# The shift inside the softmax exponentials of an attention kernel: an immediate 4 in place of a column per head

## The chip, the cores and the metric

The kernel runs on one core of a Trainium2 chip, as one launch. The metric is the device time of that launch in microseconds. The engines of the core are named as in the profile: PE (TensorE, matrix multiplications), PEld (its weight loads), ACT (ScalarE, activations), DVE (VectorE), POOL (GpSimd) and SP (SyncE, which here only issues DMAs). SBUF is the working memory, 128 partitions wide; PSUM, in 8 banks of 128x512 fp32, is what PE writes to.

## The reference

Two blocks read the same x (2048 tokens of 1024 numbers) and a gate mixes them:

```python
g = _sigmoid((x * gate_w).sum(-1, keepdims=True))
a = _A_ref(x, A_wqkv, A_wo)          # attention, 32 heads of 32 numbers
b = _B_ref(x, B_w_q, B_k1, B_k2, B_u, B_v)   # a router over 64 experts
return g * a + (1 - g) * b
```

The part that matters here is the attention:

```python
scores = jnp.einsum("bhqd,bhkd->bhqk", q, k) * (Dh ** -0.5)
p = _softmax(scores, axis=-1)
o = jnp.einsum("bhqk,bhkd->bhqd", p, v)
```

A softmax does not change when the same number is taken from all scores of a row. The kernel takes no maximum of the scores: it computes exp(score - shift) with a shift known ahead, adds the rows up, and divides by the sum at the end.

## The kernel before

All is fp32. The stages run one after the other: projections to q and k, router, projections to v (up to some 645 us of the span), attention (to some 1840 us), output projection (to the end). The scheduling is by hand: the order of the Python calls is the order of each engine's queue.

**The shift and the branch.** While q and k are evacuated, `evac` keeps the greatest absolute value of each of their rows in `amax`. The products of the two, spread by head over columns (`prf`), are summed over a head's 32 rows by a product with ones in `bound` (L450 to L455): the sum bounds every score of the head, before the scale. `bound` writes this bound, times minus the scale, into a column per head of `shift`, on all 128 partitions: four matmuls fill the four groups of 32 partitions, and an ACT copy scales them. It also writes the greatest bound of all heads to `cbits`. At the end of the program (L1456) `cbits` is loaded into a register and compared, as bits, with a limit: if a bound is above 30 after the scale, `exact` computes the attention again with true maxima. With the reference's inputs the greatest bound is 2.77, or 0.49 after the scale (worked out from the inputs).

**The attention loop** (L1083) makes 16 steps for each of the 32 heads. A step calls `unit(h, i)`, a chunk of 512 queries times four blocks of 128 keys:

- `score` issues 12 PE matmuls (L819), four at a time in different row groups of the array, into four banks of a ring of seven PSUM banks (`ring`).
- `weigh` issues the ACT exponentials (L825) from the ring into the SBUF tiles `P`. A unit has 2048 columns: two exponentials of 512 and one of 1024, or four of 512 where the ring wraps inside the last pair. This is the instruction whose bias operand is `shift[:, h:h + 1]`.
- `pv` multiplies one earlier P tile by V (L940), two steps late. At step 2 of a head it is left out, and `head_sums` puts the row sums of the head before the last one into a ring bank instead (L950), from where DVE copies them (L987, `ssb`); step 3 then makes two `pv`.

There are eight P buffers, used in turn, and each step takes one more, so a P tile must be free again about 6.5 steps after it is full. Until then `pv` has read it, and its row sums have been taken along. `presum` does that in one of two ways: DVE adds the tile to an accumulator (`acc`, L964 and L966), or, for three tiles of each head, POOL issues a DMA that adds it to a second accumulator in SBUF (`accd`, L959). In most heads tile 1 is the second accumulator itself, and tiles 6, 11 and 15 are added to it, each such DMA after the one before has landed. `merge` (L969) adds the two accumulators, 6 steps into the next head.

**The queue of SP** carries, in this order within a head: the store of the finished head's output (`od`, after the ACT copy `osb`, L980), the store of row sums (`smd`, after the DVE copy `ssb`), eight loads of K and Q for the next head (256 KB each, onto 32 partitions each), and a load of V; in heads 8 to 23 two 128-partition loads of `wo` too. Once in four heads, `load_r` reads the row sums of the four heads back (`rr`), and at step 8 `norm_r` on DVE takes their reciprocals (L998 to L1000) and SP stores them (`rd`). A head with `norm_r` in the queue of DVE, together with the head after it, is called a turn below: heads 5 and 6, 9 and 10, and so on, seven times in the loop.

Of the kernel before, what the change touches and what calls it, by code (L numbers as in the profile page):

```python
# [9 lines left out]
F32 = mybir.dt.float32  # L10
F32R = mybir.dt.float32r
I32 = mybir.dt.int32
AF = mybir.ActivationFunctionType
# [5 lines left out]
H = 32  # L19
# [5 lines left out]
W = 256  # L25
SCALE = 32 ** -0.5

SHIFT_LIMIT = 30.0


@with_exitstack
def gated_mha_peer_kernel(ctx, tc, xT, wqkv, wv, wo, wq, k12, ug, v, out):
# [8 lines left out]
    nc = tc.nc  # L41
# [3 lines left out]
    const = ctx.enter_context(tc.tile_pool(name="const", bufs=1))  # L45
# [19 lines left out]
    ones = const.tile([128, 32], F32, name="ones")  # L65
    nc.vector.memset(ones, 1.0)
    G64 = const.tile([128, 64], F32, name="G64")
    cbits = const.tile([1, 1], F32, name="cbits")
    shift = const.tile([128, H], F32, name="shift")


    const.tile([128, 56], F32, name="fill")
# [32 lines left out]
    def bank():  # L105
        i = bank_no[0] % 8
        bank_no[0] += 1
        return ps1.tile([128, 512], F32, name=f"bk{i}")
# [215 lines left out]
    for k, (w, c) in enumerate(chunks):  # L324
        hi, lo = whl.pop((w, c))
        for n in range(NQ):
            ps = bank()
# [44 lines left out]
    prf = prm.rearrange("p c j -> p (c j)")  # L372
# [76 lines left out]

    def bound():  # L450
        pb = bank()
        for i in range(4):
            nc.tensor.matmul(pb[32 * i:32 * i + 32, :H], ones, prf, start=True, stop=True)
        nc.vector.tensor_reduce(cbits, pb[:1, :H], axis=AX.X, op=OP.max)
        nc.scalar.activation(shift, pb[:, :H], AF.Copy, scale=-SCALE)  # L455

    def gate_sums():
        pz = bank()
# [26 lines left out]
    for t in range(NT - 1):  # L485
        router_mm(t)
        router_step(t)
        if t == 4:
            bound()
            load_wv(0, "xh0")  # L490
            load_wv(1, "xl0")
        if t == 5:
            gate_sums()
            rz.close()
        if t >= 8 and t % 2 == 0:
            ni, ki = divmod(t // 2 - 4, 2)
            in_parts(f"B{ki + 1}{2 - ni}", x_place(f"x{'hl'[ki]}{1 + ni}"), WR[ki, 1 - ni])
# [244 lines left out]
    def values_unit(u):  # L742
# [10 lines left out]
        for k, name in enumerate(order):  # L753
# [6 lines left out]
            if last and name == "P2":  # L760
                first_scores()
# [42 lines left out]
    P, pools = {}, {}  # L804

    def p_tile(h, kt):

        i = pools["next"] % 8
        pools["next"] += 1
        P[h, kt] = pools["left" if i >= 4 else "right"].tile([128, S], F32, name=f"P{i}")  # L810
        return P[h, kt]

    def score(K, Q, p, c, banks, on=lambda ins, *_: ins):

        for i in range(3):
            for r in range(4):
                k0, q0 = 1024 * (i == 2) + 128 * p, 1024 * (i == 1) + 512 * c
                rows = slice(32 * r, 32 * r + 32)
                on(nc.tensor.matmul(banks[r], K[rows, k0:k0 + 128], Q[rows, q0:q0 + 512],  # L819
                                    start=(i == 0), stop=(i == 2)), r)  # L820

    def weigh(h, tiles, c, r, m, src):

        dst = tiles[r // 2].rearrange("p (b s) -> p b s", b=2)[:, r % 2:r % 2 + m, 512 * c:512 * c + 512]
        return nc.scalar.activation(dst, src, AF.Exp, bias=shift[:, h:h + 1], scale=SCALE)  # L825

    def first_scores():

        tp.close()
        pools.update(right=Pool("ppr", side="right"), next=0)  # L830
        tiles = [p_tile(0, i) for i in range(2)]
        banks = [ps1.tile([128, 512], F32, name=f"bk{i}") for i in (5, 6, 0, 1)]
        score(*Z, 0, 0, banks)
        for r, ps in enumerate(banks):
            weigh(0, tiles, 0, r, 1, ps[:, None, :])

    def pv_bank():
        return pso.tile([128, 512], F32, name="o")
# [41 lines left out]
    ring = pss.tile([128, NB, 512], F32, name="ring")  # L880
# [3 lines left out]
    def ring_banks(n):  # L884
        i = [(ring_no[0] + k) % NB for k in range(n)]
        ring_no[0] += n
        return i

    def on_ring(ins, *banks):

        for other, theirs in users:
            if ins.ins.engine != other.ins.engine and not theirs & set(banks):
                tc.declare_no_dep(ins.ins, other.ins, reason="different banks of the ring")
        users.append((ins, set(banks)))
        del users[:-18 * NB]
# [19 lines left out]
    def unit(h, i):  # L915


        m, c = divmod(i, 2)
        banks = ring_banks(4)
        score(*KQ[h % 2], m, c, [ring[:, k, :] for k in banks], lambda ins, r: on_ring(ins, banks[r]))  # L920
        for p in (2 * m, 2 * m + 1):
            if c == 0 and p == sums_of(h)[0]:
                P[h, p] = ACCD[h] = wk.tile([128, S], F32, name="accd")
            elif c == 0:
                p_tile(h, p)
        cuts = sorted({1, 2, 4} | {r for r in range(1, 4) if banks[r] == 0})
        r0 = 0
        for r1 in cuts:
            k = banks[r0]
            on_ring(weigh(h, [P[h, 2 * m], P[h, 2 * m + 1]], c, r0, r1 - r0, ring[:, k:k + r1 - r0, :]),  # L930
                    *range(k, k + r1 - r0))
            r0 = r1

# [10 lines left out]
    def sums_of(h):  # L944
        return (2, 4, 6) if h == H - 1 else (2, 6, 11, 15) if h == 0 else (1, 6, 11, 15)
# [117 lines left out]
    for k in range(2 * KC):  # L1063
        c = slice(k % 2 * D // 2, (k % 2 + 1) * D // 2)
# [18 lines left out]
    for s in range(H * NT):  # L1083
        h, i = divmod(s, NT)
        if s > 0:
            unit(h, i)
        if h >= 2 and i == LAG - 1:
            head_sums(h - 2)
        elif s + 1 >= LAG:
            for _ in range(1 + (h >= 2 and i == LAG)):  # L1090
                next_pv()
        if h == H - 1 and i == 8:
            head_sums(h - 1)
        for f, a in todo.pop(s, []):
            f(*a)
        if i % 2:
            for p in (i - 1, i):
                presum(h, p)
# [240 lines left out]
    for n in range(2, S // W):  # L1339
        unit(n)  # L1340
# [112 lines left out]
        gps.close()  # L1453
        gate.close()

    limit_bits = int(np.float32(SHIFT_LIMIT / SCALE).view(np.int32))  # L1456
    creg = nc.values_load(cbits.bitcast(I32), min_val=0, max_val=2 ** 31 - 1,
                          skip_runtime_bounds_check_because="a float's bits without its sign")
    with tc.If(creg > limit_bits):
# [29 lines left out]
```

## Time and profile before

| | |
|---|---|
| median of 3 runs | 2027.85 us (2026.49 to 2029.06) |
| the profiled execution | 2027.6 us, of which the span (first to last instruction) is 2025.8 us |
| granted TensorE clock, mean | 0.995 |
| PE busy | 1974.6 us, 97% |
| ACT busy | 1338.1 us, 66% |
| DVE busy | 1384.6 us, 68% |
| POOL busy | 171.1 us, 8% |
| exponentials into P from the ring (L825) | x1530, 1074.4 us |
| exponentials into accd from the ring (L825) | x77, 84.5 us |

How to read the lines quoted below: a group line gives the source line, the engine, the operation, what is written and read, the shapes, the count, then busy time in us, the mean duration of one in ns, and the idle time of the engine just before them with what ended it. A timeline line gives the start in us of the span, the time to the end of the merged instructions, the engine, the line and the count; in brackets stands idle time before it and what ended it. Durations of consecutive ACT instructions overlap, so the rate of ACT is read from their starts. A window line gives, for a stretch of the span, its length, the busy time of each engine (with its count of instructions), the granted clock, the mean busy share of the 16 DMA engines (it may pass 1, since a packet's time includes some waiting) and GB/s.

### The profile page before, as it was taken

Reading aid. Unit: us, or ns where it says so; the run is one execution under the profiler, and the core shown is the slowest. Engines: PE = TensorE matmul, PEld = TensorE weight load, DVE = VectorE, ACT = ScalarE, POOL = GpSimd, SP = SyncE. Lnnn points to the kernel's source line nnn. Section 1 sums busy time; section 2 is a strip of 40 time slices with the busy share of each in tenths; the row PEclk is TensorE's granted clock in tenths of the full one; section 3 lists DMA queues with packets and bytes.
Section 4 is the critical chain, followed back from the end, with each engine's and each line's share of the span. In section 5 each row is a group of like instructions: output and inputs, shape, how many; then the busy total and the mean of one; then the engine's idle time right before and its main releaser. Section 6 shows DMA issues by size and latency. Waiting matters only on the chain. (4 is left out here: it accounts for less than half of the span.)

```text
span 2025.8 us, 34915 instructions
## 1 busy us (share of the span) xinstructions
PE 1974.6 (97%) x14227; PEld 1079.8 (53%) x14227; DVE 1384.6 (68%) x1254; ACT 1338.1 (66%) x1973; POOL 171.1 (8%) x218
## 2 busy tenths in 40 slices
PE   9999999999999999999999999999999999999998
PEld 7877778878886333333333333333333333336786
DVE  4522227779867777687688688678688688677574
ACT  4211112112333999999999999989999999995221
POOL 0000000055011000000000000000000000001000
PEclk9999999999999999999999999999999999999999
DMA  5777754221377878878778789778788787875961
GB/s 197 272 277 278 270 210 143 93 84 58 127 237 242 168 143 170 154 152 169 152 164 174 154 166 172 152 167 170 149 175 159 156 169 159 158 161 164 277 184 54
DMA packets 125361, 348.47 MB, mean 172 GB/s; under 512 B 16852, under 2 KB 57188, under 8 KB 99464
## 3 DMA queue, kind: packets, MB, share of 16 engines
q1 hardware_dynamic: 86680, 195.40, 36.3%
q0 software_dynamic: 17904, 112.99, 27.5%
q10 hardware_dynamic: 20608, 37.76, 5.2%
q8 instruction: 114, 1.87, 0.4%
q14 instruction: 55, 0.45, 0.1%
HBM read 174.90 MB, written 71.57 MB: 122 GB/s over the span
## 5 line engine op out<-in xcount | busy, mean ns | idle before, releaser
L825 ACT ACTIVATE P<-ring,shift 128x512 f32<-128x512 f32 (+1 forms) x1530 | 1074.4, 914 | 50.8 <-issue 23.1
L966 DVE TENSOR_TENSOR acc<-acc,P 128x2048 f32<-128x2048 f32 x319 | 731.0, 2292 | 74.9 <-ACT P L825 51.6
L940 PE MATMUL o<-P,V 128*32 128x512 f32 x3840 | 515.2, 608 | 2.5 <-DMA V<-vd 1.4
L819 PE MATMUL ring<-z,z 32*128 32x512 f32 x3060 | 324.8, 441 | 23.6 <-DVE ssb L987 15.9
L819 PE MATMUL ring<-Q,K 32*128 32x512 f32 x3072 | 322.5, 438 | 10.4 <-ACT P L825 8.5
L819 PEld LDWEIGHTS ring<-z,z 32*128 32x128 f32 x3060 | 169.8, 185 | 282.3 <-ACT P L825 119.2
L819 PEld LDWEIGHTS ring<-Q,K 32*128 32x128 f32 x3072 | 169.1, 183 | 266.9 <-ACT P L825 123.2
L95 ACT ACTIVATE hi<-bk 128x512 fp32r<-128x512 f32 x64 | 37.6, 599 | 242.9 <-PE bk L331 231.2
L331 PE MATMUL bk<-xh,whi 128*128 128x512 f32 x448 | 176.3, 394 | 0.1
L331 PE MATMUL bk<-xh,wlo 128*128 128x512 f32 x448 | 174.6, 390 | 0.0
L331 PE MATMUL bk<-xl,whi 128*128 128x512 f32 x448 | 174.6, 390 | 0.0
L959 POOL DMA_DIRECT2D accd<-P x95 | 81.5, 858 | 1089.7 <-ACT P L825 817.3
L940 PEld LDWEIGHTS o<-P,V 128*32 128x32 f32 x3840 | 76.2, 108 | 180.8 <-issue 164.9
L96 DVE TENSOR_TENSOR lo<-bk,hi 128x512 fp32r<-128x512 f32 x64 | 44.1, 690 | 182.2 <-ACT hi L95 178.5
L964 DVE TENSOR_TENSOR acc<-P,P 128x2048 f32<-128x2048 f32 x32 | 73.3, 2291 | 70.3 <-ACT P L825 64.5
L331 PEld LDWEIGHTS bk<-xh,whi 128*128 128x128 f32 x448 | 84.1, 188 | 24.1 <-issue 6.7
L331 PEld LDWEIGHTS bk<-xh,wlo 128*128 128x128 f32 x448 | 84.1, 188 | 17.6
L331 PEld LDWEIGHTS bk<-xl,whi 128*128 128x128 f32 x448 | 84.2, 188 | 16.8
L825 ACT ACTIVATE accd<-ring,shift 128x1024 f32<-128x1024 f32 (+1 forms) x77 | 84.5, 1142 | 0.0
L969 DVE TENSOR_TENSOR acc<-acc,accd 128x2048 f32<-128x2048 f32 x32 | 73.2, 2286 | 1.8 <-DMA accd<-P 1.8
L987 DVE COPY ssb<-ring 128x512 f32<-128x512 f32 x31 | 21.4, 690 | 72.6 <-ACT osb L980 62.6
L564 PE MATMUL pa<-woh,acc 128*128 128x512 f32 x192 | 62.6, 391 | 1.1 <-ACT acc L95 0.8
(242 smaller groups left out, 1858.7 us busy)
## 6 DMA issues: line engine op xcount, KB each, us to landing
accd<-P POOLq DMA_DIRECT2D x95, 1024.0 KB, 8.3
wqt<-in_wq SPq DMA_DIRECT2D x32, 1024.0 KB
z<-kd SPq DMA_DIRECT2D x64, 256.0 KB
z<-qd SPq DMA_DIRECT2D x64, 256.0 KB
K<-kd SPq DMA_DIRECT2D x64, 256.0 KB
Q<-qd SPq DMA_DIRECT2D x64, 256.0 KB
V<-vd SPq DMA_DIRECT2D x32, 256.0 KB
od<-osb SPq DMA_DIRECT2D x32, 256.0 KB
```

Of the source, the lines that this page charges most:

```text
L95: nc.scalar.activation(hi, src, AF.Copy)
L96: (on or nc.vector).tensor_tensor(out=lo, in0=src, in1=hi.bitcast(F32), op=OP.subtract)
L331: nc.tensor.matmul(ps, a[:, kc, :], b[n][:, kc, :], start=first, stop=last)
L564: nc.tensor.matmul(ps, self.a[a][i][:, k, :], self.b[b][j][k], start=(not first and k == 0 and i == j == 0), stop=(k == HC - 1 and i == 1))
L819: on(nc.tensor.matmul(banks[r], K[rows, k0:k0 + 128], Q[rows, q0:q0 + 512], start=(i == 0), stop=(i == 2)), r)
L825: return nc.scalar.activation(dst, src, AF.Exp, bias=shift[:, h:h + 1], scale=SCALE)
L940: nc.tensor.matmul(O[h][32 * qc:32 * qc + 32, :], Vt[g][:, kt, 32 * j:32 * j + 32], P[h, p][:, qc * 512:(qc + 1) * 512], start=(p == 0), s ...
L959: nc.gpsimd.dma_start(ACCD[h], P[h, kt], accum_op=OP.add)
L964: nc.vector.tensor_add(ACC[h], P[h, 0], P[h, kt])
L966: nc.vector.tensor_add(ACC[h], ACC[h], P[h, kt])
L969: nc.vector.tensor_add(ACC[h], ACC[h], ACCD[h])
L987: ins = copy(o, ps)
```

## The change

The exponentials take the immediate -4 as their bias for every head. The tile `shift` (128 bytes per partition) is gone, with the ACT copy that filled it and three of the four matmuls in `bound`; the one left makes only row 0, which `cbits` needs. The limit that the branch at the end tests is 4 after the scale, in place of 30. Since the bound is 0.49, the branch is not taken before or after the change.

```diff
-SHIFT_LIMIT = 30.0
+SHIFT = 4.0
...
-    shift = const.tile([128, H], F32, name="shift")
...
     def bound():
         pb = bank()
-        for i in range(4):
-            nc.tensor.matmul(pb[32 * i:32 * i + 32, :H], ones, prf, start=True, stop=True)
+        nc.tensor.matmul(pb[:1, :H], ones[:, 0:1], prf, start=True, stop=True)
         nc.vector.tensor_reduce(cbits, pb[:1, :H], axis=AX.X, op=OP.max)
-        nc.scalar.activation(shift, pb[:, :H], AF.Copy, scale=-SCALE)
...
-    def weigh(h, tiles, c, r, m, src):
+    def weigh(tiles, c, r, m, src):
...
-        return nc.scalar.activation(dst, src, AF.Exp, bias=shift[:, h:h + 1], scale=SCALE)
+        return nc.scalar.activation(dst, src, AF.Exp, bias=-SHIFT, scale=SCALE)
...
-            weigh(0, tiles, 0, r, 1, ps[:, None, :])
+            weigh(tiles, 0, r, 1, ps[:, None, :])
...
-            on_ring(weigh(h, [P[h, 2 * m], P[h, 2 * m + 1]], c, r0, r1 - r0, ring[:, k:k + r1 - r0, :]),
+            on_ring(weigh([P[h, 2 * m], P[h, 2 * m + 1]], c, r0, r1 - r0, ring[:, k:k + r1 - r0, :]),
...
-    limit_bits = int(np.float32(SHIFT_LIMIT / SCALE).view(np.int32))
+    limit_bits = int(np.float32(SHIFT / SCALE).view(np.int32))
```

## The prediction

> **What bounds the kernel now.** I read the page first, then the groups by shape, then the timelines of ACT, PE and POOL inside the attention loop, then the stretches of one head.
>
> ```profile
> span 2025.8 us, 34915 instructions
> PE 1974.6 (97%) x14227; PEld 1079.8 (53%) x14227; DVE 1384.6 (68%) x1254; ACT 1338.1 (66%) x1973; POOL 171.1 (8%) x218
> ACT  4211112112333999999999999989999999995221
> ```
>
> PE is busy in all stages, but a busy PE may be one that waits inside. ACT is nearly full in 23 of the 40 slices only, and these are the attention loop. The change touches its exponentials, so the loop is the stage to read. The exponentials by shape:
>
> ```profile
> L825 ACT ACTIVATE P<-ring,shift 128x512 f32<-128x512 f32 x1144 | 761.7, 805 | 50.8 <-issue 23.1 <-ACT P L825 14.5 <-DMA accd<-P 7.0
> L825 ACT ACTIVATE P<-ring,shift 128x1024 f32<-128x1024 f32 x386 | 477.6, 1237 | 0.0
> L825 ACT ACTIVATE accd<-ring,shift 128x1024 f32<-128x1024 f32 x51 | 66.2, 1298 | 0.0
> L825 ACT ACTIVATE accd<-ring,shift 128x512 f32<-128x512 f32 x26 | 18.3, 837 | 0.0
> ```
>
> That is 1170 of 512 columns and 437 of 1024. Their mean durations include time behind the one before, so the price of one is read from start to start:
>
> ```profile
> 757.35 1.16 ACT L825 ACTIVATE accd<-ring,shift 128x1024 f32<-128x1024 f32 x1
> 758.35 1.33 ACT L825 ACTIVATE P<-ring,shift 128x512 f32<-128x512 f32 x2
> 759.49 1.34 ACT L825 ACTIVATE accd<-ring,shift 128x512 f32<-128x512 f32 x2
> 760.63 0.69 ACT L980 ACTIVATE osb<-o 128x512 f32<-128x512 f32 x1
> 761.11 1.37 ACT L825 ACTIVATE P<-ring,shift 128x512 f32<-128x512 f32 x2
> ```
>
> An exponential of 1024 takes 1.00 us (757.35 to 758.35), one of 512 takes 0.57 (two in 758.35 to 759.49, two more to 760.63). The Copy `osb`, same shape, also from PSUM to SBUF, but with immediates only, takes 0.48 (760.63 to 761.11). So ACT needs (1170 x 0.57 + 437 x 1.00) / 32 + 0.48 = 35.0 us per head.
>
> PE in a step at the pace of ACT, and then in the steps of another head after ACT has caught up:
>
> ```profile
> 1001.58 1.24 PE L819 MATMUL ring<-Q,K 32*128 32x512 f32 x12
> ...
> 1003.74 1.38 PE L819 MATMUL ring<-Q,K 32*128 32x512 f32 x12
> ```
> ```profile
> 797.55 1.06 PE L950 MATMUL ring<-acc,ones 128*32 128x512 f32 x8
> 798.55 0.50 PE L819 MATMUL ring<-z,z 32*128 32x512 f32 x2
> ...
> 800.78 1.06 PE L940 MATMUL o<-P,V 128*32 128x512 f32 x8
> 801.66 1.04 PE L940 MATMUL o<-accd,V 128*32 128x512 f32 x8
> 802.63 0.97 PE L819 MATMUL ring<-z,z 32*128 32x512 f32 x12
> 803.53 1.06 PE L940 MATMUL o<-P,V 128*32 128x512 f32 x8
> 804.53 0.98 PE L819 MATMUL ring<-z,z 32*128 32x512 f32 x12
> ```
>
> A step at ACT's pace takes 2.16 us (1001.58 to 1003.74); a free step takes 1.90 (802.63 to 804.53), 0.90 for the scores and 1.00 for `pv`. PE's own need per head is 16 x 0.90 + 14 x 1.00 + 1.00 (the sums, 797.55 to 798.55) + 1.85 (the two `pv` of step 3, 800.78 to 802.63) = 31.25 us. Now the actual length of a head, from the accumulating DMAs that POOL issues, and the restart of ACT:
>
> ```profile
> 811.72 0.86 POOL L959 DMA_DIRECT2D accd<-P  x1 [14.70 <-ACT P L825]
> 826.26 0.86 POOL L959 DMA_DIRECT2D accd<-P  x1 [13.69 <-DMA accd<-P]
> 833.73 0.86 POOL L959 DMA_DIRECT2D accd<-P  x1 [6.61 <-ACT P L825]
> 848.43 0.86 POOL L959 DMA_DIRECT2D accd<-P  x1 [13.84 <-ACT P L825]
> ...
> 887.35 0.86 POOL L959 DMA_DIRECT2D accd<-P  x1 [15.83 <-ACT P L825]
> ...
> 923.63 0.86 POOL L959 DMA_DIRECT2D accd<-P  x1 [15.71 <-ACT P L825]
> ```
> ```profile
> 825.84 2.27 ACT L825 ACTIVATE P<-ring,shift 128x512 f32<-128x512 f32 x3 [0.31 <-DMA accd<-P]
> ```
>
> The issues at 811.72, 848.43, 887.35 and 923.63 are those of tile 6 in four heads. Two of the three distances are regular, 36.7 and 36.3 (I take 36.5); the middle one, 38.9, is a turn. A head thus takes 1.5 us over ACT's 35.0: ACT is the bound, with small waits. One of them is a warning. At 825.84, step 14, ACT had waited for the DMA of tile 6, issued at 811.72: its buffer is the one that step 14 writes. That wait is 0.31 us now, so this DMA lands just when the present pace needs it.
>
> **The change part by part.** *The exponentials.* Each loses its operand in SBUF: 0.57 - 0.48 = 0.09 us, if Exp and Copy differ in nothing else. 1607 x 0.09 = 145 us of ACT, 4.5 per head, leaves 30.5. ACT is then below PE's 31.25, so at most 36.5 - 31.25 = 5.2 us of a head can be won. The ends: if the difference belongs to Exp and not to the column, the saving is 0; above 0.075 (3.75 us over 50 exponentials of a head) PE is the bound and more brings nothing. I take 0.09, since shape, source and destination are the same in both rows.
>
> *What is late next: DVE.* Adds per head:
>
> ```profile
> L966 DVE TENSOR_TENSOR acc<-acc,P 128x2048 f32<-128x2048 f32 x319 | 731.0, 2292 | 74.9 <-ACT P L825 51.6 <-DVE acc L966 0.9
> ...
> L964 DVE TENSOR_TENSOR acc<-P,P 128x2048 f32<-128x2048 f32 x32 | 73.3, 2291 | 70.3 <-ACT P L825 64.5 <-PE ring L950 3.1 <-DMA vd<-xh 2.8
> L969 DVE TENSOR_TENSOR acc<-acc,accd 128x2048 f32<-128x2048 f32 x32 | 73.2, 2286 | 1.8 <-DMA accd<-P 1.8
> ```
>
> (731.0 + 73.3 + 73.2) / 32 = 27.4 us, under 31.25: no bound in a regular head.
>
> *What is late next: the DMAs.* One head, from a landing of tile 6 (restart at 825.84) to the next one:
>
> ```profile
> 825.80:835.00 9.20, 9.01 (x84) 3.33 (x80) 5.64 (x3) 9.16 (x14) 1.71 (x2) 1.00 0.56 114
> 835.00:845.00 10.00, 9.66 (x92) 3.41 (x88) 6.58 (x4) 9.31 (x15) 0.00 (x0) 1.00 1.01 213
> 845.00:855.00 10.00, 10.00 (x100) 4.03 (x97) 7.68 (x4) 10.00 (x15) 0.86 (x1) 1.00 1.06 190
> 855.00:862.20 7.20, 7.20 (x69) 2.62 (x68) 0.00 (x0) 7.20 (x11) 0.00 (x0) 1.00 0.55 105
> ```
>
> The share times the length adds up to 5.2 + 10.1 + 10.6 + 4.0 = 29.8 us of full engines per head, close to PE's 31.25. And it cannot be packed evenly: after a landing, the DMAs of tiles 11 and 15 go one after the other (826.26, 833.73), 8 us at a share of 0.56 that no faster ACT shortens. After these 8 us the remaining 29.8 - 4.5 = 25.3 run at 1.03 at best (the two middle rows): 24.5 us, so a head of 32.5. If the thin tail of 7.2 us at 0.55 stays too, it costs 3.2 more: 35.7.
>
> The landing of tile 6 from its issue: now the issue comes 848.43 - 825.84 = 22.6 us after the restart. ACT has nine and a half steps and an `osb` in between, 9.5 x 30.0 / 16 + 0.5 = 18.3 us in the future, PE about 19 (nine steps at 1.90, the sums, the double `pv`). So the issue moves to about 19 us, ahead of some of the loads of K, Q and V that it follows today. With today's 14.1 us to landing (811.72 to 825.84) that gives a head of 33.1. I take 33.7 for a regular head, between this and the middle of the two bounds (34.1): **2.8 us less, in 24 heads, 67 us.**
>
> [...]
>
> *A turn.* DVE stands before the reciprocals, and PE's ring bank waits for DVE:
>
> ```profile
> 862.25 0.20 DVE L998 TENSOR_SCALAR rr<-rr 128x64 f32<-128x64 f32 x1 [9.46 <-DMA rr<-smd]
> ...
> 877.74 0.69 DVE L987 COPY ssb<-ring 128x512 f32<-128x512 f32 x1
> ```
> ```profile
> 878.48 0.96 PE L819 MATMUL ring<-z,z 32*128 32x512 f32 x10 [2.51 <-DVE ssb L987]
> ```
>
> `rr` lands with the accumulation (862.25), and 16.2 us of queued DVE adds pass until PE goes on (878.48); neither gets shorter. Of the other 22.7 us some eight and a half steps shrink by 0.26: **2.2 us, in 7 turns, 15 us.**
>
> *The last head* has its accumulations early (tiles 4 and 6); 18 steps and the drain at 0.26 give **5 us**. *The rest*:
>
> ```profile
> L453 PE MATMUL bk<-prm,ones x8: 196/207/218, 419.5 to 419.6; 128*32 128x32 f32 x8
> ```
>
> Six of these eight passes go, all within 0.3 us, and an ACT Copy of 32 columns; **0.4 us** at most, nothing at least. The tiles behind `shift` lie 128 bytes lower; no row prices that, and I take 0. The branch costs the same, as it isn't taken.
>
> Sum: 2027.6 - 67 - 15 - 5 - 0.4 = 1940 us, against the profiled execution, which lies 0.25 us under the median.
>
> **The rivals.** *PE alone is the bound* (the accumulation, issued early, lands in time): a regular head 31.7 with a little friction, 4.8 us less in 24; a turn 3.5 less; 5 at the end: 2027.6 - 115 - 25 - 5 = 1882. For it: free steps of 1.90 do occur; against: 29.8 us of DMA in 31.7.
>
> *The accumulation's landing is pinned* 36.4 us after the one before, whatever the issue: 0.1 to 0.3 us in 24 heads, 15 in the turns, 5 at the end: 2027.6 - 5 - 20 = 2003. For it: the restart at 825.84 shows ACT on that DMA already, and all 16 engines are full from 835 to 855; against: its issue moves ahead of loads.
>
> *Slower: every head becomes a turn.* The output's store then comes 1.1 us earlier after a landing, beside the DMA of tile 15; if this one lands so late that `merge` blocks DVE for over 6 us, DVE's queue holds the ring bank as at 877.74, and a regular head takes 38.9: 24 x 2.4 = 58 us more, 5 less at the end, 2080. Against: `merge` has waited for it 1.8 us in total.
>
> *The change doesn't do what it says* (the -4 still comes from a column): 2027.
>
> A longer wait also touches the clock:
>
> ```profile
> 1328.00:1332.00 4.00, 4.00 (x28) 1.26 (x28) 2.12 (x2) 2.46 (x4) 0.00 (x0) 0.56 0.98 236
> ```
>
> After a turn's wait the granted clock was 0.56 for 4 us. [...]
>
> **How the numbers follow.** Forecast 0.50 (1915 to 1970: heads of 32.5 to 35), PE alone 0.19, pinned 0.23, no effect 0.03, slower 0.05. The range from 1885 to 2003 reaches both neighbours. About 4 us (0.2%) can be told from no change: faster 0.92, the same 0.03, slower 0.05.
>
> **What would show it.** Exponentials 0.48 us from start to start (0.91 for 1024); ACT's idle time going from `issue` to the DMA of `accd`; tile 6 issued some 19 us after a landing; a regular head of 33.7; steps of 1.90 on PE. I am wrong if the exponentials keep 0.57, if heads are 31.7 with no wait on `accd`, or if tile 6 lands 36 us after the one before.

## The result, and the profile after

The changed kernel takes 1977.1 us (median of 4 runs, 1974.5 to 1980.7), the kernel before 2028.5 us (median of 4): a ratio of 0.975, with a 95% interval of 0.973 to 0.977. 51 us were won; 88 had been forecast, with a range of 1885 to 2003. The profiled execution of after took 1980.73 us with a span of 1978.9 us, 46.9 us less than the profiled execution of before.

The head of the page of after, then the share of the chain of waits by what it ran through:

```profile
span 1978.9 us, 34902 instructions
PE 1894.2 (96%) x14221; PEld 1023.2 (52%) x14221; DVE 1384.7 (70%) x1254; ACT 1201.4 (61%) x1972; POOL 171.2 (9%) x218
ACT  4211112101423898978988888888889888895221
...
DMA accd<-P 11%; PE ring L816 10%; PE o L937 9%; PE pa L561 6%; DVE acc L963 4%; DMA rr<-smd 4%; ACT P L822 3%; DMA z<-kd 2%; PE ring L947 1%; DMA od<-osb 1%; DMA wo_raw<-t1l 1%; DMA accd<-rd 1%; PE pa L1136 1%; DMA smd<-ssb 0%; ACT accd L822 0%
```

ACT is busy 1201 us in place of 1338, 137 us less, and is no longer full in the loop. The chain's largest part is now the DMA that adds to `accd`. The exponentials in the timeline of ACT:

```profile
784.99 1.11 ACT L822 ACTIVATE accd<-ring 128x1024 f32<-128x1024 f32 x1
785.89 1.19 ACT L822 ACTIVATE P<-ring 128x512 f32<-128x512 f32 x2
786.85 1.15 ACT L822 ACTIVATE accd<-ring 128x1024 f32<-128x1024 f32 x1
787.75 0.74 ACT L977 ACTIVATE osb<-o 128x512 f32<-128x512 f32 x1
788.23 4.07 ACT L822 ACTIVATE P<-ring 128x512 f32<-128x512 f32 x6
```

One of 1024 columns takes 0.90 us (784.99 to 785.89, and 786.85 to 787.75), one of 512 takes 0.48 (two in 785.89 to 786.85), as long as the Copy `osb` (787.75 to 788.23). The saving of 0.09 us is there in full. What ACT does with it shows in the groups, where the first idle time is now the DMA's:

```profile
L822 ACT ACTIVATE P<-ring 128x512 f32<-128x512 f32 (+1 forms) x1530 | 939.1, 766 | 144.9 <-DMA accd<-P 61.1
```

Before, 7.0 us of ACT's waits in the loop were for that DMA; now it is 61.1. One head in the timelines of POOL and ACT, from a restart to the next one:

```profile
800.38 0.86 POOL L956 DMA_DIRECT2D accd<-P  x1 [11.14 <-ACT P L822]
815.38 0.86 POOL L956 DMA_DIRECT2D accd<-P  x1 [14.14 <-DMA accd<-P]
822.74 0.86 POOL L956 DMA_DIRECT2D accd<-P  x1 [6.50 <-ACT accd L822]
835.15 0.86 POOL L956 DMA_DIRECT2D accd<-P  x1 [11.56 <-ACT P L822]
```
```profile
814.96 3.90 ACT L822 ACTIVATE P<-ring 128x512 f32<-128x512 f32 x6 [1.62 <-DMA accd<-P]
...
849.56 5.03 ACT L822 ACTIVATE P<-ring 128x512 f32<-128x512 f32 x8 [2.34 <-DMA accd<-P]
```

Tile 6 is issued at 800.38 and 835.15, a head of 34.8 us. From the restart at 814.96 to the issue are 20.2 us (22.6 before), from the issue to the next restart, at 849.56, 14.4. There are 30 such waits of ACT in the loop, and in most heads PE waits with it. By their place in the loop 22 are for tile 6, at step 14, and 8 for tile 15 of the head before, at step 8; the longest of the 30, 4.5 us, is one of these 8.

The stretches from one issue of tile 6 to the next, for seven of the thirty heads; after the length come the busy times of PE, PEld, DVE, ACT and POOL, then the granted clock, the DMA share and GB/s:

```profile
835.15:877.36 42.21, 36.10 (x332) 12.38 (x328) 29.33 (x18) 31.44 (x51) 2.57 (x3) 0.92 0.80 169
877.36:909.57 32.21, 32.21 (x340) 11.17 (x332) 27.35 (x13) 31.20 (x53) 2.57 (x3) 1.00 0.76 162
909.57:944.73 35.16, 32.61 (x332) 11.31 (x328) 28.02 (x14) 31.18 (x52) 2.58 (x4) 1.00 0.78 142
944.73:979.22 34.49, 33.25 (x332) 11.60 (x330) 28.10 (x14) 31.36 (x53) 2.58 (x3) 1.00 0.84 175
...
1051.12:1087.53 36.41, 34.09 (x336) 11.70 (x332) 28.08 (x14) 31.37 (x53) 2.57 (x3) 0.95 0.80 169
...
1195.82:1234.87 39.05, 35.05 (x332) 12.06 (x331) 27.74 (x14) 31.53 (x53) 2.57 (x4) 0.91 0.82 175
...
1411.86:1454.20 42.34, 37.31 (x332) 12.56 (x328) 29.43 (x18) 31.62 (x52) 2.57 (x3) 0.88 0.80 169
```

The lengths go with the clock. Of the 23 regular heads, 16 ran at a full clock and took 33.5 us on average: nine of about 34.5 like 944.73, six that follow a turn and take about 32.3 like 877.36 (in five of them PE is busy from end to end), and the loop's first, of 31.3. Six heads with a clock of 0.95 took 36.4 on average, and one with 0.91 took 39.1. In before, all 23 regular heads had a clock of 1.00 and took 36.3. The seven turns took 40.5 us (40.0 before), at clocks between 0.88 and 0.96.

How a head loses its clock, in PE's timeline of one regular head, and the clock of the stretches around it:

```profile
1063.89 0.50 PE L816 MATMUL ring<-Q,K 32*128 32x512 f32 x3
1066.71 1.09 PE L816 MATMUL ring<-Q,K 32*128 32x512 f32 x9 [2.32 <-ACT P L822]
1067.73 1.94 PE L937 MATMUL o<-P,V 128*32 128x512 f32 x8
1069.59 1.51 PE L816 MATMUL ring<-z,z 32*128 32x512 f32 x12
```
```profile
1064.00:1067.40 3.40, 1.08 (x12) 0.56 (x12) 3.30 (x2) 1.34 (x3) 0.86 (x1) 1.00 0.15 46
1067.40:1070.80 3.40, 3.40 (x25) 1.04 (x20) 2.47 (x2) 2.56 (x4) 0.00 (x0) 0.50 0.93 193
```

PE waits 2.32 us for ACT, which waits for the DMA. From 1067.40 on the clock is 0.50 for 3.4 us: a `pv` that takes 1.00 us elsewhere takes 1.86 (1067.73 to 1069.59). In a turn it is worse:

```profile
861.66 0.50 PE L816 MATMUL ring<-z,z 32*128 32x512 f32 x2
866.39 1.65 PE L816 MATMUL ring<-z,z 32*128 32x512 f32 x10 [4.24 <-DVE ssb L984]
867.97 1.94 PE L937 MATMUL o<-P,V 128*32 128x512 f32 x8
869.83 1.65 PE L816 MATMUL ring<-z,z 32*128 32x512 f32 x12
871.41 1.75 PE L937 MATMUL o<-P,V 128*32 128x512 f32 x8
873.09 0.97 PE L816 MATMUL ring<-z,z 32*128 32x512 f32 x12
```

The wait for `ssb` is 4.24 us where it was 2.51, and the two steps behind it take 3.44 and 3.26 us in place of 1.90: 2.9 us lost. In the record of the clock the loop of after has 17 such stretches, 75 us in all; the loop of before has 3, 14 us in all.

### The profile page after: what moved, and what is told of

Same layout as the page of the kernel before. It is cut to its first block, busy times and chain, and to the rows that moved or that the text cites. A ratio compares the mean times of both kernels' runs of the same rounds, so it can differ in the third digit from the quotient of the medians.

```text
span 1978.9 us, 34902 instructions
## 1 busy us (share of the span) xinstructions
PE 1894.2 (96%) x14221; PEld 1023.2 (52%) x14221; DVE 1384.7 (70%) x1254; ACT 1201.4 (61%) x1972; POOL 171.2 (9%) x218
## 3 DMA queue, kind: packets, MB, share of 16 engines
q1 hardware_dynamic: 86680, 195.40, 36.1%
## 4 chain that ended last, share of the span: by engine, by line
PE 27%; DMA 19%; DVE 5%; ACT 3%; issue 2%; SPq 0%; DVEq 0%; ACTq 0%; POOLq 0%
DMA accd<-P 11%; PE ring L816 10%; PE o L937 9%; PE pa L561 6%; DVE acc L963 4%; DMA rr<-smd 4%; ACT P L822 3%; DMA z<-kd 2%; PE ring L947 1%; DMA od<-osb 1%; DMA wo_raw<-t1l 1%; DMA accd<-rd 1%; PE pa L1136 1%; DMA smd<-ssb 0%; ACT accd L822 0%
## 5 line engine op out<-in xcount | busy, mean ns | idle before, releaser
L822 ACT ACTIVATE P<-ring 128x512 f32<-128x512 f32 (+1 forms) x1530 | 939.1, 766 | 144.9 <-DMA accd<-P 61.1
L937 PE MATMUL o<-P,V 128*32 128x512 f32 x3840 | 528.6, 623 | 2.7 <-DMA V<-vd 1.8
L816 PE MATMUL ring<-z,z 32*128 32x512 f32 x3060 | 281.1, 443 | 35.2 <-DVE ssb L984 19.3
L816 PE MATMUL ring<-Q,K 32*128 32x512 f32 x3072 | 277.1, 434 | 31.3 <-ACT P L822 31.1
L816 PEld LDWEIGHTS ring<-z,z 32*128 32x128 f32 x3060 | 141.8, 191 | 284.2 <-ACT P L822 138.3
L816 PEld LDWEIGHTS ring<-Q,K 32*128 32x128 f32 x3072 | 139.6, 186 | 274.1 <-ACT P L822 153.5
L822 ACT ACTIVATE accd<-ring 128x1024 f32<-128x1024 f32 (+1 forms) x77 | 72.3, 973 | 0.0
L984 DVE COPY ssb<-ring 128x512 f32<-128x512 f32 x31 | 21.4, 689 | 62.0 <-PE ring L947 48.1
```

What stands on the lines that cost most here:

```text
L822: return nc.scalar.activation(dst, src, AF.Exp, bias=-SHIFT, scale=SCALE)
L937: nc.tensor.matmul(O[h][32 * qc:32 * qc + 32, :], Vt[g][:, kt, 32 * j:32 * j + 32], P[h, p][:, qc * 512:(qc + 1) * 512], start=(p == 0), s ...
L984: ins = copy(o, ps)
```

## The experiments

Medians are of four to seven executions each (one in the last two runs), ratios against the kernel before on the same chip (2027.4, 2028.8 and 2029.3 us).

### Is it the immediate, or one of the other edits?

The kernel after, with the -4 in a column of 128 rows that is set once:

```diff
+    shift = const.tile([128, 1], F32, name="shift")
+    nc.vector.memset(shift, -SHIFT)
...
-        return nc.scalar.activation(dst, src, AF.Exp, bias=-SHIFT, scale=SCALE)
+        return nc.scalar.activation(dst, src, AF.Exp, bias=shift, scale=SCALE)
```

> The changed kernel with all its edits but one: the bias of the exponentials comes from a column of -4 in SBUF, filled once by a memset. Theory (the immediate alone makes the difference; the value of the shift, the smaller bound() and the limit nothing): 2024 to 2032 us, as the kernel before. Rival (the value, the addresses or bound() take part): below 2015 us.

2034.3 us, ratio 1.002 (1.000 to 1.004). The whole gain is gone although everything else of the change stayed: the new limit of the branch and the smaller `bound` win nothing.

### Is the accumulating DMA the new bound?

The kernel after (first run) and the kernel before (second run) without the three DMA additions of each head. The row sums of those tiles are left out of the computation.

```diff
         if kt in sums:
-            nc.gpsimd.dma_start(ACCD[h], P[h, kt], accum_op=OP.add)
             return
```

> The changed kernel without the DMAs that add tiles 6, 11 and 15 of each head (4 and 6 of the last) to the second accumulator: their row sums are left out of the output's divisor. Theory (after the change a head waits for the landing of tile 6, since the DMA engines are full): the waits go and a head falls from some 35 us to PE's need of 31.25 and a little, the time to 1860 to 1895 us. Rival (the wait for the landing only stands where PE, the clock or ACT would have made another one): 1955 to 1980 us.

> The kernel before, with the column, without the same DMAs (the same row sums are left out). Theory (ACT is the bound of the kernel before, at 35.0 us a head): 1965 to 2000 us, so that between this one and the one without a column lie 90 us or more, against 51 with the DMAs in place. Rival (DMAs were already the bound before): it falls to within 60 us of the one without a column.

Without them after takes 1863.8 us (0.919, interval 0.917 to 0.920) and before 1996.2 (0.984, 0.983 to 0.986). With no DMA to wait for, the immediate is worth 132 us, close to the 145 us of ACT that it saves; with the DMAs it is worth 51. The additions cost the kernel before 31 us and the kernel after 113.

The mean granted clock of after without them is 0.998 (0.979 with them), and 1.00 over its loop (640 to 1680). Its heads take 32.1 us, not the 31.25 that I had added up for PE. Step 3 in PE's timeline, and PE's weight loads there:

```profile
777.50 1.06 PE L947 MATMUL ring<-acc,ones 128*32 128x512 f32 x8
778.50 1.88 PE L816 MATMUL ring<-z,z 32*128 32x512 f32 x12
780.31 1.07 PE L937 MATMUL o<-P,V 128*32 128x512 f32 x8
781.19 1.04 PE L937 MATMUL o<-accd,V 128*32 128x512 f32 x8
782.16 0.97 PE L816 MATMUL ring<-z,z 32*128 32x512 f32 x12
```
```profile
778.93 0.18 PEld L816 LDWEIGHTS ring<-z,z 32*128 32x128 f32 x1 [0.24 <-ACT P L822]
779.42 0.52 PEld L816 LDWEIGHTS ring<-z,z 32*128 32x128 f32 x9 [0.31 <-ACT P L822]
```

The scores of step 3 take 1.81 us (778.50 to 780.31), since their banks come free one exponential at a time; I had given them the 0.90 of a free step.

### Does the DMA land at a fixed time, or a fixed time after its issue?

Two runs. In the first, every second unit of the kernel after gets the column, so that ACT's gain is halved:

```diff
+    shift = const.tile([128, 1], F32, name="shift")
+    nc.vector.memset(shift, -SHIFT)
...
-    def weigh(tiles, c, r, m, src):
+    def weigh(tiles, c, r, m, src, bias=-SHIFT):
...
-        return nc.scalar.activation(dst, src, AF.Exp, bias=-SHIFT, scale=SCALE)
+        return nc.scalar.activation(dst, src, AF.Exp, bias=bias, scale=SCALE)
...
-            on_ring(weigh([P[h, 2 * m], P[h, 2 * m + 1]], c, r0, r1 - r0, ring[:, k:k + r1 - r0, :]),
+            on_ring(weigh([P[h, 2 * m], P[h, 2 * m + 1]], c, r0, r1 - r0, ring[:, k:k + r1 - r0, :],
+                          shift if i % 2 else -SHIFT),
```

> The changed kernel with the bias from a column of -4 in every second unit, an immediate in the others: ACT needs 32.8 us a head in place of 30.5. Theory (a head of the changed kernel takes 35 us for its DMAs, so ACT has over 2 us to spare): 1975 to 1990 us. Rival (ACT's rate still sets the time): halfway, 2003 us.

2003.7 us, ratio 0.987 (0.985 to 0.989): half of the pace brings half of the gain. The theory that the landing is pinned and ACT's second half is only time to spare fell here. In its place: the loop of a head is two parts in series, from one landing of tile 6 to the next issue of tile 6, which follows the pace (medians of 30 heads: 23.7 us with the column, 22.4 with half, 21.4 with none; in the shortest, those without a wait on the way, 22.4, 21.1 and 20.2), and from the issue to the landing, which does not (medians of 31, in the same order: 13.7, 13.5 and 14.1).

In the second run half of the loads of K and Q are left out from the third head on, so that those heads multiply what an earlier one left there:

```diff
-        for r in range(4):
+        for r in range(4 if h < 2 else 2):
             dma(K[32 * r:32 * r + 32, :], k[r // 2])
```

> The changed kernel with half of the loads of K and Q (rows 0 to 63 of each) left out from the third head on; those heads compute with older rows. Theory (the addition of tile 6 lands some 14.5 us after its issue because it shares the DMA engines with these loads, and a head is the way from a restart to that issue, 20 us, plus that landing): the landing comes by some 10 us or less and a head goes to 32 or 33 us, 1865 to 1900 us. Rival (the chain of the three additions itself is slow, or another wait takes over): over 1940 us.

1867.3 us, ratio 0.921 (0.919 to 0.923), a clock of 0.997, and POOL's timeline:

```profile
790.49 0.86 POOL L956 DMA_DIRECT2D accd<-P  x1 [15.02 <-ACT P L822]
799.08 0.86 POOL L956 DMA_DIRECT2D accd<-P  x1 [7.73 <-ACT P L822]
...
822.66 0.86 POOL L956 DMA_DIRECT2D accd<-P  x1 [14.73 <-ACT P L822]
```

Tile 11 follows tile 6 by 8.6 us (by 15.0 in the head of after shown above, 800.38 to 815.38) and waits for ACT, no longer for the DMA before it. From issue to landing tile 6 takes 8.8 us in the median, in place of 14.1. Heads take 32.2 us (790.49 to 822.66). So it is the loads that make the accumulation long here, and with half of them it hides.

### What does the turn cost?

The reciprocals go to the end of their head:

```diff
-            at(base + 2 * NT + 8, norm_r, g)
+            at(base + 2 * NT + 15, norm_r, g)
```

> The changed kernel with the reciprocals of the row sums (norm_r) at step 15 of their head in place of step 8, behind the landing that they wait for, so that DVE goes on with its adds. Theory (a turn costs some 3 us over a regular head through DVE's blocked queue): 7 x 2 to 4 us less, 1950 to 1965 us. Rival (the DMAs take the same time in a turn whatever DVE does): 1972 to 1980 us.

1967.6 us (1954.1 to 1968.8), ratio 0.968 (0.964 to 0.972), between the two theories. The turns are gone: those seven heads take 34.8 us in place of 40.5, 40 us in sum. But the regular ones take 35.4 in place of 34.5, so that of the 40 us 18 are left in the sum of the thirty heads, 14 between the profiled executions, and 10 between the medians. Two of its heads:

```profile
1012.95:1049.17 36.22, 34.03 (x332) 11.63 (x328) 28.05 (x14) 31.24 (x51) 2.57 (x3) 0.95 0.86 185
...
1473.77:1508.66 34.89, 32.73 (x336) 11.27 (x328) 28.09 (x14) 31.27 (x53) 2.57 (x4) 1.00 0.86 175
```

The relation is that of after: 11 regular heads with a full clock take 34.1 us, nine with one halved stretch 36.1, three with two 38.2. With no turn before them, the heads of 32 are gone as well, and 12 of the 23 regular heads have a halved stretch, where 7 had. Its four executions say the same without any edit between them: 1954.1 us at a mean clock of 0.989, the three others 1967.0 to 1968.8 at 0.981 to 0.984.

### Can the DMAs be placed better?

Three additions, moved to tiles 9, 11 and 15:

```diff
-        return (2, 4, 6) if h == H - 1 else (2, 6, 11, 15) if h == 0 else (1, 6, 11, 15)
+        return (2, 4, 6) if h == H - 1 else (2, 9, 11, 15) if h == 0 else (1, 9, 11, 15)
```

> Nothing left out: the changed kernel with the same three DMA additions per head, but tile 9 in place of tile 6: it has 8 steps (15.2 us) until its buffer is written again in place of 6.5 (12.3 us), and its issue lies behind most of the loads. Theory (the distance to reuse is what is short, not the DMA engines' total): 1900 to 1945 us. Rival (the engines' total of 29.8 us per head in 32 is too much, wherever the additions stand): 1960 to 1985 us.

2006.1 us, ratio 0.990 (0.988 to 0.993): both theories missed. Two lines of its waits in the loop, with the total, the count and the longest:

```profile
ACT P L822 <- DMA accd<-P: 93.7, 20, 8.8
DVE acc L966 <- DMA accd<-P: 83.8, 18, 8.7
```

ACT's waits are fewer than in after (20 for 30) and over twice as long (4.7 us on average for 2.0). The wait of step 14 has gone, but the chain of three additions, each after the one before, now ends in the loads of the next head; there `merge` and step 8 wait for tile 15, which lands 12.6 us after its issue in the median (10.8 in after). The clock is 0.971, the lowest of all runs.

Two additions, tiles 9 and 15, with one more tile a head added by DVE; nothing is left out. First with the late reciprocals as above, then with them in their old place, then the same arrangement (late reciprocals) in the kernel before:

```diff
-        return (2, 4, 6) if h == H - 1 else (2, 6, 11, 15) if h == 0 else (1, 6, 11, 15)
+        return (2, 4, 6) if h == H - 1 else (2, 9, 15) if h == 0 else (1, 9, 15)
```

> Nothing left out: the changed kernel with two DMA additions per head in place of three, tiles 9 and 15 (DVE adds the third tile), and with norm_r at step 15. Theory (waits for a landing and blocked turns make all of the 113 us over the run without additions; tiles 9 and 15 have 8 steps until reuse in place of 6.5, and a third of that DMA work is gone; DVE's need rises to 12.97 x 2.29 + 0.69 = 30.4 us, or 31.7 with a gap of 0.1 us behind each add, just under 32.1): 1865 to 1900 us. Rival (DVE becomes the bound or the landing is late all the same): 1920 us or more.

> The kernel of e7 with norm_r back at step 8: only the DMA additions differ from the changed kernel (two per head, tiles 9 and 15). Theory (the landings make most of the 113 us, and with no addition between them the row sums land early, so that a turn blocks DVE less): 1864 to 1885 us. Rival (a turn costs its 5 us over a regular head whatever the additions): 1895 to 1905 us.

> The kernel before, with the column, in the arrangement of e7 (two DMA additions per head, tiles 9 and 15, norm_r at step 15). Theory (with the landings out of the way the column costs what ACT needs more, 36.1 against 32.1 us a head): 1985 to 2000 us, some 130 us over e7. Rival (the arrangement helps the column as much): under 1950 us.

1864.0 us (0.920, 0.918 to 0.922), 1863.3 (0.919, 0.917 to 0.921) and 1994.9 (0.983, 0.981 to 0.985). POOL's timeline of the first of them, two issues of tile 9:

```profile
794.08 0.86 POOL L956 DMA_DIRECT2D accd<-P  x1 [19.80 <-ACT P L822]
...
826.12 0.86 POOL L956 DMA_DIRECT2D accd<-P  x1 [19.81 <-ACT P L822]
```

The head is 32.0 us long (32.1 in the median of all), as fast as with no addition at all; ACT waits for no DMA in these heads, and the clock is 0.999. This version beats both kernels, by 8.0% (the ratio above) and by 5.7% (1864.0 / 1977.1). The late reciprocals add nothing to it. In this arrangement the immediate is worth 131 us (1994.9 - 1864.0), as without the DMAs.

### Why do the router's matmuls change?

See the last section; the kernel after, with an unused constant of 128 bytes per partition, or of 64, where `shift` had been:

```diff
+    const.tile([128, 32], F32, name="pad")
```

> The kernel after, with one unused constant tile of 128 bytes a partition (32 columns of fp32) in the place of the column that the change took out. Theory that the place of the router's operands in SBUF sets the pace of its matmuls: the 384 router matmuls of lines 395 and 396 go back from 390-391 ns to 395-397 ns, the loop over heads starts 2 to 3 us later (644-646 us), time 1977 to 1984 us. Rival, that it is the bias column of the exponential, as something that is read, that does it: 390-391 ns, loop at 641-643 us, time 1974 to 1981 us.

> The kernel after, with one unused constant tile of 64 bytes a partition. Theory that any shift of the addresses does it: 395-397 ns for the router's matmuls, as with 128 bytes. Rival, that only some shifts do it (a boundary of more than 64 bytes): 390-391 ns here, loop at 641-643 us.

Both give the router's matmuls 395 to 397 ns, as in before: the theory of the addresses held, and 64 bytes do as much as 128. One execution each, 1987.7 and 1975.4 us, with the loop's halved clock in them: two or three us cannot be read from these times, and 1987.7 lies above the 1977 to 1984 that was expected.

## Why the prediction was right, and where its size was off

The time of 1977 us lies inside the range, but above the 1915 to 1970 that the forecast itself stood for: what happened is the forecast's mechanism with a cost that it put at nothing.

**Exponentials, ACT, the bound: right.** 0.09 us each was forecast, and 0.57 went to 0.48, 1.00 to 0.90. The column alone undid it (2034.3 us). ACT was the bound of before, shown by the 132 us when nothing else stands in the way.

**What is late next: right in its kind.** Tile 6 was to be awaited in every head, with an issue some 19 us after the restart and 14.1 us to the landing. It is 20.2 and 14.4 in the head shown. Of the 1.2 us, 0.9 is step 3 of PE: 1.81 us for its scores in the run without additions. My own rows of before showed 2.23 there (798.55 to 800.78), and I counted 0.90 for them, as in a free step. The eight waits for tile 15, 15 us in sum, I had not priced: a late landing of that tile stood only in the rival *slower*.

**The regular head: right at a full clock, and the clock was the mis-sized term.** I wrote 33.7 us; the 16 heads at a full clock take 33.5. That close a match is partly luck: it is the mean of nine heads of 34.5, which wait for the landing as I drew it, and of seven shorter ones, six of them behind a turn, that my sum did not have. The 14.1 us from issue to landing, which I had from one head of before, came out in the median. The other seven heads take 36.8. The sums of the profiled executions, from issues of tile 6:

| | forecast gain, us | measured |
|---|---|---|
| up to the first issue | 0.4 | 2.0 |
| regular heads | 67 (24) | 42.3 (23: 835.7 to 793.4) |
| turns | 15 (7) | -3.5 (7: 279.8 to 283.2) |
| from the last issue to the end | 5 | 6.1 |
| sum | 88 | 46.9 |

What is missing in the regular heads is mostly the clock: against the 34.5 of a full-clock head that follows no turn, six heads lost 1.9 us and one 4.6, 16 us. One halved stretch of 3.4 us costs 1.7 us of PE's work, two cost 3.4: this explains the 1.9 and most of the 4.6.

**The turns: wrong in sign.** The 16.2 us from `rr` to PE's restart came out as I took them (850.16 to 866.39). But PE, now faster, arrived earlier at the same wait, 4.24 us in place of 2.51, and its clock was halved behind it. By the clocks of the seven stretches a turn loses 3.2 us to the throttle where it lost 1.0 before: 2.2 of the 2.7 us by which the forecast missed each turn. Regular heads and turns together, the clock takes some 32 of the 41 us that are missing. The record of the clock gives the same size: half of the 75 us of halved stretches in the loop, less half of the 14 before, is 31.

**The step that failed** is thus the price of the clock: the sum has no term for it. I had taken the waits of a regular head, some 2.5 us in all, as too short to bring the clock down. No run shows that they are: six regular heads at a clock of 0.95 lost 1.9 us each. The row of 0.56 in 1328 to 1332 has a wait of 2.30 us ahead of it in PE's timeline of before:

```profile
1322.28 0.50 PE L819 MATMUL ring<-z,z 32*128 32x512 f32 x2
1325.08 1.65 PE L819 MATMUL ring<-z,z 32*128 32x512 f32 x10 [2.30 <-DVE ssb L987]
1326.66 1.94 PE L940 MATMUL o<-P,V 128*32 128x512 f32 x8
```

The clock was halved behind it, while four of the seven turns of before, with waits of 2.14 to 2.51 us, have no halved stretch behind them. In after, the 17 halved stretches follow waits of PE of 1.9 to 4.2 us, 13 of them under 3 us. Another wait of 2.55 us was followed by none, as its row and the next one, 0.89 us later at the usual pace, show:

```profile
925.30 0.96 PE L816 MATMUL ring<-Q,K 32*128 32x512 f32 x9 [2.55 <-ACT P L822]
926.19 1.07 PE L937 MATMUL o<-P,V 128*32 128x512 f32 x8
```

So the length alone does not decide. The record of the clock in the trace of after shows what comes closer. The 17 stretches last 3.41 or 6.83 us and begin on a grid of 3.413 us: from 746.55 to 866.01 are 35 such pieces, from there to 1009.37 another 42. In each piece of the loop that runs at a full clock, add up the time in which no matmul runs. The 17 pieces just ahead of a halved stretch have 1.65 us of it or more (2.32 in the window from 1064.00 above), and no other piece has more than 1.63; in before, 1.94 and more stand against 1.61 and less. The wait of 2.55 us falls into two pieces, with 1.28 and 1.27 us:

```profile
920.63:924.04 3.41, 2.13 (x23) 0.57 (x19) 3.31 (x2) 1.01 (x2) 0.00 (x0) 1.00 0.26 55
924.04:927.46 3.42, 2.15 (x21) 0.92 (x25) 2.44 (x2) 2.80 (x5) 0.86 (x1) 1.00 0.38 81
```

Two traces show this and no more. Of waits of 2.30 and 2.55 us the first was followed by half the clock and the second was not; a wait of 1.9 us or more must thus be priced as one that can halve the clock.

That the halved clock costs the time, and does not only go with longer heads, is shown in part: the two steps that run at half are on the path from the restart to the issue, and their loss is measured (2.9 us behind the wait of 4.24); executions of one kernel differ in time as their clocks do (with the late reciprocals 1954.1 us at 0.989, 1967.0 to 1968.8 at 0.981 to 0.984); and where PE hardly waits, the clock stays: after the change, with none of the additions or with two and the late reciprocals, PE is idle for 3.9 and 4.1 us of the 1040 from 640 to 1680, at a clock of 1.00 there, while after, with all its additions, has 70 of 1155 (640 to 1795), at 0.97. A run that keeps the waits and the clock both was not tried.

**The rivals.** PE alone (1882): not in after as a whole; heads at PE's pace came only in the six behind a turn, and in all heads once the DMAs gave way, at 1864. Pinned (2003): fell, since half a column brings half the gain. Every head a turn: did not come, as regular heads fell from 36.3 to 34.5 on average. No effect: fell with the exponentials.

**Addresses at nothing: wrong by some 2 to 3 us**, on the gaining side; the next section.

## What to carry to other kernels

A bias column costs 0.09 us per activation here, at 512 and at 1024 columns about alike (0.57 against 0.48 us, 1.00 against 0.90), so a constant that can be an immediate should be one; but count what is in series behind the freed engine, because the head's loop (exponentials up to a tile, then a DMA beside the loads) let through 51 of 132 us until the DMA was moved and one of three given to DVE. When a change gathers PE's small waits into one of 1.9 us or more, read the granted clock behind such waits in the trace that you have, and price the halved steps (1.7 us of PE's work for 3.4 us at 0.50 here). Sum PE's need step by step from rows of the same step, not from a free step.

## What the runs showed of the hardware

The router's matmuls, which the change doesn't touch, became faster by about 1.4%. One of its three groups by shape, in before and then in after:

```profile
L396 PE MATMUL bk<-wph,xl 128*128 128x512 f32 x128 | 50.6, 395 | 0.0
```
```profile
L395 PE MATMUL bk<-wph,xl 128*128 128x512 f32 x128 | 49.9, 390 | 0.0
```

In after with 128 or with 64 bytes of padding the group reads as in before. Between 390 and 395 to 397 ns, 384 such matmuls make some 2 us, and the first exponential starts at 644.31 us in after, at 647.11 in before, at 647.06 with 128 bytes of padding and at 647.99 with 64. It is not the size of `shift` as such: a column of 4 bytes (2034.3 us above) gives 396 to 397 ns as well. Where tiles lie in SBUF thus changes the pace of these matmuls by a per cent or so. Whether it is the place of their own operands or of what other engines use meanwhile, and by which rule, these runs do not tell.
